# Accumulating kv = phi(k)ᵀ v per head on 32-column PE tiles instead of per pair of heads on 64-column tiles

## Chip, cores, metric

One core of one Trainium2 chip. The metric is the device time in microseconds of one execution, as a median over runs; 2% is the line between "same" and a difference. A *pair* below is a weight load and its matmul; *entry* is the time from the start of the last matmul ahead of a block to the first start in it.

## The reference, cut to what matters

A gated mix of a linear-attention block (2048 tokens, 32 heads of 32) and a feed-forward on one selected row. The change touches this part:

```python
pq, pk = phi(q), phi(k)                       # phi(t) = where(t > 0, t + 1, exp(t)) + 1e-6
kv = jnp.einsum("bhsd,bhse->bhde", pk, v)     # per head: 32 x 32, summed over 2048 tokens
z  = jnp.einsum("bhsd->bhd", pk)              # per head: the sum of phi(k)
num = jnp.einsum("bhqd,bhde->bhqe", pq, kv)
den = jnp.einsum("bhqd,bhd->bhq", pq, z)[..., None] + 1e-6
```

z comes for free when v carries a column of ones.

## The kernel before

Tokens are taken in 16 tiles of 128. For each, k and v are projected (512-column matmuls, `unit_KV`), k goes through phi into `pk`, v into `vt`. Every fourth tile, the sums of four tiles of tokens are added up in one block (`unit_KVACC` four times):

```python
def kv_slot(g):                                    # g: 8 groups of 4 heads
    return kvacc[g // 4][:, 65 * (g % 4) : 65 * (g % 4) + 65]
...
vt_t[t] = kvp.tile([P, NG, 2, 65], BF, tag="vt", name=f"vt{t}")
nc.gpsimd.memset(vt_t[t][:, :, :, 64:65], 1.0)
...
def unit_KVACC(t):
    for g in range(NG):
        for h in range(2):                         # two heads at once, on a 64-column tile
            pe.matmul(kv_slot(g)[64 * h : 64 * h + 64, :], lhsT=pk_t[t][:, g * P + 64 * h : g * P + 64 * h + 64],
                      rhs=vt_t[t][:, g, h, :], start=False, stop=False, skip_group_check=True, tile_position=(0, 64 * h))
    del pk_t[t], vt_t[t]
...
for t in range(4):
    unit_KVACC(t)
for t in range(4, NT):
    for nb in range(4):
        unit_KV(t, nb)
        if nb == 1 and t > 4 and t % 4 == 0:
            for t0 in range(t - 4, t):
                unit_KVACC(t0)
        ffn_step(GU_AFTER.get((t, nb), 0))         # gate/up matmuls of the selected row, 32-column tiles
```

Two heads share a matmul, so half of each 64x64 product (head a's k with head b's v) is computed and never used. Each matmul has its own weight load (`lhsT`), so a block is 64 pairs of load and matmul. Just ahead of the first block stands `rps`, the router (32 matmuls on 32-column tiles); after the third stand gate/up matmuls, after the fourth `yps`, all on 32-column tiles.

## Time and profile before

| | before |
|---|---|
| time | 251.35 us (250.92 to 251.53) |
| TensorE busy | 244.6 us of 251.4 |
| four kv blocks in the chain | 4 x 1.14 us |
| matmuls and weight loads into `kvacc` | 256 and 256 |

The prediction below shows the lines that say so.

The timeline of DVE after the last block (start, length, engine, operation, out<-in, shapes, count):

```profile
159.04 0.22 DVE L80 COPY zcol<-kvacc 128x4 f32<-128x4 f32 x2
159.18 0.42 DVE L80 CAST kvbd<-kvacc 128x256 bf16<-128x256 f32 x1
...
159.97 0.42 DVE L80 TENSOR_TENSOR zc<-mzc,zcol 128x256 bf16<-128x256 f32 x1
...
160.47 0.36 DVE L80 CAST kvbd<-kvacc 128x256 bf16<-128x256 f32 x1
```

These five operations bring the sums out of PSUM. The first reader of `zc` starts at 162.3 us.

### The profile page before, as it was taken

The page shows a single profiled execution, that of the slowest core. Times are in us where ns is not written, and L with a number is a line of the kernel's source. Part 1 is how long each engine was busy: PE and PEld are TensorE (multiplying, and loading weights), DVE is VectorE, ACT ScalarE, POOL GpSimd, SP SyncE. Part 2 cuts the span into 40 slices and gives each one's busy share as a digit, 9 for nine tenths or more (in the row PEclk, how much of TensorE's full clock was granted, in tenths as well). Part 3 has the DMA queues.
Part 4 walks back from the last instruction along what each step waited for, and adds up shares of the span by engine and source line. Part 5 has one row for each costly group of instructions (what it writes and reads, how often), then busy time and mean ns, then how long its engine had stood idle before and what let it go on. Part 6 is the DMA issues. An engine that isn't in the chain of part 4 may idle for free.

```text
span 251.4 us, 4171 instructions
## 1 busy us (share of the span) xinstructions
PE 244.6 (97%) x1576; PEld 112.0 (45%) x1602; DVE 163.3 (65%) x257; ACT 125.7 (50%) x200; POOL 51.8 (21%) x102
## 2 busy tenths in 40 slices
PE   8999999999999999999999999999999999999994
PEld 3444445444444534444544444444444444444442
DVE  0036005244999469699699993585888999953442
ACT  2068334455455355545535644568888633333210
POOL 5000002010000100000033000210666689950000
PEclk9999999999999999999999999999999999999999
DMA  6999990008999992489699996130000564454122
GB/s 191 308 344 215 258 341 18 0 5 269 356 348 287 331 288 68 146 297 328 215 310 314 429 349 146 52 132 7 4 0 0 158 220 146 152 183 139 71 83 83
DMA packets 47242, 47.73 MB, mean 190 GB/s; under 512 B 18732, under 2 KB 35380, under 8 KB 47160
## 3 DMA queue, kind: packets, MB, share of 16 engines
q1 hardware_dynamic: 46552, 46.29, 60.2%
q0 software_dynamic: 640, 1.19, 1.6%
q8 instruction: 12, 0.20, 0.3%
q14 instruction: 6, 0.05, 0.1%
q10 hardware_dynamic: 32, 0.00, 0.0%
HBM read 39.34 MB, written 8.40 MB: 190 GB/s over the span
## 4 chain that ended last, share of the span: by engine, by line
PE 95%; DMA 2%; issue 1%; SPq 0%; DVE 0%; DVEq 0%
PE ps L80 87%; PE first L80 3%; DMA xnat<-in_A_x_dram 2%; PE kvacc L80 2%; PE dps L80 1%; PE rps L80 1%; PE pm L80 1%; PE pst L80 0%; PE gps L80 0%; SPq L80 0%; DVE ot L80 0%; PE yps L80 0%; PE xs_ps L80 0%; DVEq L747 0%; PE pt L80 0%
## 5 line engine op out<-in xcount | busy, mean ns | idle before, releaser
L80 PE MATMUL ps<-wkv,xT 128*128 128x512 bf16 x468 | 105.6, 379 | 0.6
L80 PEld LDWEIGHTS <-xT 128*128 128x128 bf16 x512 | 49.9, 99 | 60.9 <-issue 3.0
L80 PE MATMUL ps<-xT,wq 128*128 128x512 bf16 x248 | 57.5, 379 | 0.7 <-issue 0.5
L80 PE MATMUL ps<-m_sb,pq_all 128*128 128x512 bf16 (+2 forms) x259 | 55.3, 372 | 0.3
L80 ACT ACTIVATE u<-ps 128x512 f32<-128x512 f32 x60 | 35.8, 597 | 36.8 <-PE ps L80 36.1
L80 ACT ACTIVATE e<-u 128x512 f32<-128x512 f32 x64 | 40.3, 630 | 2.0
L650 POOL TENSOR_TENSOR pq_all<-pq_all,rb 128x512 bf16<-128x512 bf16 x32 | 36.6, 1172 | 14.4 <-DVE rb L80 14.0
L80 PEld LDWEIGHTS <-pq_all 128*128 128x128 bf16 x264 | 25.5, 98 | 30.2 <-issue 0.4
L80 PEld LDWEIGHTS <-wq 128*128 128x128 bf16 x256 | 24.3, 98 | 30.2 <-issue 2.1
L80 DVE SCALAR_TENSOR_TENSOR pq_all<-ps,e 128x512 bf16<-128x512 f32 x32 | 21.9, 686 | 23.8 <-ACT e L80 23.7
L80 DVE SCALAR_TENSOR_TENSOR gacc<-wt,hcol,gacc 128x1024 f32<-128x1024 bf16 x27 | 34.6, 1282 | 3.8 <-DMA wt<-in_B_w_down_dram 3.3
L80 ACT CAST vt<-ps 128x512 bf16<-128x512 f32 x32 | 18.8, 587 | 31.6 <-PE ps L80 31.6
L80 DVE SCALAR_TENSOR_TENSOR ot<-ps,gate,xg 128x512 bf16<-128x512 f32 (+2 forms) x33 | 23.8, 733 | 15.0 <-PE ps L80 14.2
L80 ACT ACTIVATE xg<-xt,omg 128x1024 f32<-128x1024 bf16 x16 | 18.1, 1145 | 25.9 <-DVE ot L80 25.9
L80 DVE SCALAR_TENSOR_TENSOR pk<-ps,e 128x512 bf16<-128x512 f32 x28 | 19.1, 686 | 7.5 <-ACT e L80 7.5
L209 POOL MEMSET vt<- 128x16 bf16 x16 | 2.4, 199 | 103.2 <-PE kvacc L80 102.6
L80 DVE STREAM_SHUFFLE rb<-rdp 128x512 f32<-128x512 f32 x32 | 22.8, 746 | 0.0
L80 DVE SCALAR_TENSOR_TENSOR gacc<-wt,xs_f,gacc 128x1024 f32<-128x1024 bf16 x14 | 17.4, 1279 | 0.5 <-DMA wt<-in_B_w_gate_dram 0.5
L80 PE MATMUL first<-wkv,xT 128*128 128x512 bf16 x31 | 8.9, 443 | 0.1
L80 DVE SCALAR_TENSOR_TENSOR pk<-first,e 128x512 bf16<-128x512 f32 x4 | 2.8, 692 | 9.3 <-ACT e L80 9.3
L80 DVE CAST r_bf<-rps 128x512 bf16<-128x512 f32 x1 | 0.7, 693 | 12.5 <-PE rps L80 12.5
L80 DVE RECIPROCAL rd<-dn 128x512 f32<-128x512 f32 x2 | 6.7, 3338 | 0.0
(104 smaller groups left out, 89.3 us busy)
## 6 DMA issues: line engine op xcount, KB each, us to landing
wt<-in_B_w_down_dram SPq DMA_DIRECT2D x14, 512.0 KB, 5.5
wt<-in_B_w_gate_dram SPq DMA_DIRECT2D x8, 512.0 KB, 7.3
wt<-in_B_w_up_dram SPq DMA_DIRECT2D x8, 512.0 KB, 8.6
xt<-xp SPq DMA_DIRECT2D x16, 256.0 KB, 3.0
out_dram<-ot SPq DMA_DIRECT2D x15, 256.0 KB, 2.0
wt<-in_B_w_gate_dram SPq DMA_DIRECT2D x8, 384.0 KB, 6.9
wt<-in_B_w_up_dram SPq DMA_DIRECT2D x8, 384.0 KB, 7.6
wkv<-in_A_wqkv_dram SPq DMA_DIRECT2D x8, 256.0 KB, 5.2
```

The costliest lines, as they stand in the source:

```text
L80: inst = fn(*a, **k)
L209: nc.gpsimd.memset(vt_t[t][:, :, :, 64:65], 1.0)
L650: nc.gpsimd.tensor_tensor(sl, sl, rb[:], op=ALU.mult)
```

## The change

Its intent: compute no cross terms. Each head gets a 32-column tile of its own, four run at a time, and streams 33 columns instead of 65; 8 x 33 = 264 columns fit one PSUM bank, so the evacuation is shorter too.

```diff
-        return kvacc[g // 4][:, 65 * (g % 4) : 65 * (g % 4) + 65]
+        return kvacc[0][:, 33 * g : 33 * g + 33]
...
-            for h in range(2):
-                pe.matmul(kv_slot(g)[64 * h : 64 * h + 64, :], lhsT=pk_t[t][:, g * P + 64 * h : g * P + 64 * h + 64],
-                          rhs=vt_t[t][:, g, h, :], ..., tile_position=(0, 64 * h))
+            for h in range(4):
+                pe.matmul(kv_slot(g)[32 * h : 32 * h + 32, :], lhsT=pk_t[t][:, g * P + 32 * h : g * P + 32 * h + 32],
+                          rhs=vt_t[t][:, g, h, :], ..., tile_position=(0, 32 * h))
...
+    acc8 = kvacc[0][:, 0:264].rearrange("p (g e) -> p g e", e=33)
+    dve.tensor_tensor(zc[:], mzc[:], acc8[:, :, 32:33].to_broadcast([P, NG, 32]), op=ALU.mult)
+    dve.tensor_copy(kvbd[:], acc8[:, :, 0:32])
```

(`vt` has the shape [P, NG, 4, 33], `kvbd` [P, NG, 32], and the two copies into `zcol` and the second copy into `kvbd` go.) The price is in the loop: 128 pairs of load and matmul in a block instead of 64.

More of the change, by code (lines that the diff above doesn't have):

```diff
@@ L98 @@
     omg = keep.tile([P, NT], F32)
-    kvbd = keep.tile([P, NG, 64], BF)
+    kvbd = keep.tile([P, NG, 32], BF)
     zc = keep.tile([P, NG, 32], BF)
@@ L207, in kv_open @@
             pk_t[t] = kvp.tile([P, D], BF, tag="pk", name=f"pk{t}")
-            vt_t[t] = kvp.tile([P, NG, 2, 65], BF, tag="vt", name=f"vt{t}")
-            nc.gpsimd.memset(vt_t[t][:, :, :, 64:65], 1.0)
+            vt_t[t] = kvp.tile([P, NG, 4, 33], BF, tag="vt", name=f"vt{t}")
+            nc.gpsimd.memset(vt_t[t][:, :, :, 32:33], 1.0)
     def kv_mm(ps, t, nb, c0, c1):
@@ L219, in kv_evac @@
         else:
-            act.copy(vt_t[t][:, 4 * (nb - 2) : 4 * (nb - 2) + 4, :, 0:64], ps[:].rearrange("p (g h e) -> p g h e", g=4, h=2))
+            act.copy(vt_t[t][:, 4 * (nb - 2) : 4 * (nb - 2) + 4, :, 0:32], ps[:].rearrange("p (g h e) -> p g h e", g=4, h=4))
     def unit_KV(t, nb):
@@ L229, in unit_KVACC @@
         for g in range(NG):
-            for h in range(2):
-                pe.matmul(kv_slot(g)[64 * h : 64 * h + 64, :], lhsT=pk_t[t][:, g * P + 64 * h : g * P + 64 * h + 64],
-                          rhs=vt_t[t][:, g, h, :], start=False, stop=False, skip_group_check=True, tile_position=(0, 64 * h))
+            for h in range(4):
+                pe.matmul(kv_slot(g)[32 * h : 32 * h + 32, :], lhsT=pk_t[t][:, g * P + 32 * h : g * P + 32 * h + 32],
+                          rhs=vt_t[t][:, g, h, :], start=False, stop=False, skip_group_check=True, tile_position=(0, 32 * h))
         del pk_t[t], vt_t[t]
@@ L286 @@
     ps_acc = ph1.enter_context(tc.tile_pool(name="ps_acc", bufs=1, space=PSUM))
-    kvacc += [ps_acc.tile([P, 512], F32, name=f"kvacc{i}") for i in range(2)]
+    kvacc += [ps_acc.tile([P, 512], F32, name=f"kvacc{i}") for i in range(1)]
     ps_red = ph1.enter_context(tc.tile_pool(name="ps_red", bufs=1, space=PSUM))
@@ L593 @@
     unit_Q(*q_units.popleft())
-    zcol = keep.tile([P, NG], F32)
-    for i in range(2):
-        acc4 = kvacc[i][:, 0:260].rearrange("p (g e) -> p g e", e=65)
-        dve.tensor_copy(zcol[:, 4 * i : 4 * i + 4], acc4[:, :, 64])
-    dve.tensor_tensor(zc[:], mzc[:], zcol[:].unsqueeze(2).to_broadcast([P, NG, 32]), op=ALU.mult)
-    for i in range(2):
-        acc4 = kvacc[i][:, 0:260].rearrange("p (g e) -> p g e", e=65)
-        dve.tensor_copy(kvbd[:, 4 * i : 4 * i + 4, :], acc4[:, :, 0:64])
+    acc8 = kvacc[0][:, 0:264].rearrange("p (g e) -> p g e", e=33)
+    dve.tensor_tensor(zc[:], mzc[:], acc8[:, :, 32:33].to_broadcast([P, NG, 32]), op=ALU.mult)
+    dve.tensor_copy(kvbd[:], acc8[:, :, 0:32])
     ph1.close()
@@ L662, in unit_kvT @@
                     pe.matmul(pt[c][32 * r : 32 * r + 32, 32 * hf : 32 * hf + 32],
-                              lhsT=kvbd[32 * c : 32 * c + 32, 4 * hf + r, 32 * (c % 2) : 32 * (c % 2) + 32],
+                              lhsT=kvbd[32 * c : 32 * c + 32, 4 * hf + r, :],
                               rhs=ident[32 * c : 32 * c + 32, 32 * c : 32 * c + 32],
```

## The prediction

> **What bounds the kernel now.** I read the page from the top: busy shares, slices, the chain that ended last, then the groups of TensorE.
>
> ```profile
> PE 244.6 (97%) x1576; PEld 112.0 (45%) x1602; DVE 163.3 (65%) x257; ACT 125.7 (50%) x200; POOL 51.8 (21%) x102
> PE   8999999999999999999999999999999999999994
> PEclk9999999999999999999999999999999999999999
> PE 95%; DMA 2%; issue 1%; SPq 0%; DVE 0%; DVEq 0%
> ```
>
> TensorE works from end to end at full granted clock, and the chain is TensorE for 95% of the span; no other engine has a stretch on it except the first load and the last store. So only TensorE's own time counts, nearly one for one, and work removed from DVE, ACT or POOL is worth nothing unless TensorE had waited for it. The next lines, from the groups of TensorE by shape, say how much of it the change touches, and the chain in order of time says what that costs in wall time:
>
> ```profile
> L80 PE MATMUL ps<-wkv,xT 128*128 128x512 bf16 x468 | 105.6, 379 | 0.6
> L80 PE MATMUL kvacc<-vt,pk 128*64 128x65 bf16 x256 | 4.8, 196 | 0.0
> L80 PE MATMUL rps<-xT,wrg_pad 128*32 128x512 bf16 x32 | 1.9, 380 | 0.0
> ```
> ```profile
> 36.13 1.84 PE rps L80 x32
> 37.97 1.14 PE kvacc L80 x64
> ...
> 58.21 0.30 PE xs_ps L80 x9
> ...
> 82.15 1.14 PE kvacc L80 x64
> ...
> 123.29 1.14 PE kvacc L80 x64
> ...
> 157.11 1.14 PE kvacc L80 x64
> 158.25 0.57 PE yps L80 x8
> ...
> 165.19 0.22 PE pt L80 x32
> ```
>
> The columns are start, length, engine, tile, line and count. The accumulation of kv is four blocks of 64 matmuls, 1.14 us each, 4.56 us in all: 1.8% of the span. That is the whole stake, so even removing it altogether would not reach 2% (5.0 us). A block's 1.14 us is 17.8 ns for a matmul although one lasts 196 ns, because they are pipelined and two 64-column tiles run side by side. The single starts in the trace show it: the two of a pair start 3 to 10 ns apart, and pairs follow at 29 and 35 ns alternately (the longer after an odd head group). The block takes 1014 ns from first to last start, then some 126 ns until the next group starts. A block is entered 309 ns after the start of the matmul before it, where 512-column matmuls otherwise follow at 216 ns.
>
> **What the Trainium skill says.** "TensorEngine Tiling (Array Packing)", Instruction Overhead, gives each matmul about 60 cycles of overhead and says that one with a free dimension of 1 takes as long as one of 60, and warns against taking a tiling factor from a dimension that is already small. Here 65 columns, just above that, become 33, below it. The trace agrees in the one place that shows it: the nine 1-column matmuls into xs_ps start 25 ns apart (one gap 38).
>
> "TensorE: Matmul & The Clock Gate", Wait — 56ns, not 53.3ns?, says that start-to-start is never below about 25 ns, and that decoding in microcode takes about 62 ns for each matmul. This trace goes below both: 17.8 ns averaged over 64 matmuls into kvacc, 3 to 4 ns between matmuls of different tiles. I therefore read the 25 ns as a floor for one tile, not for the engine; no row here shows it for a 32-column tile.
>
> "TensorEngine Tiling (Array Packing)", Key Properties, says that changing the tiling mode drains TensorE. The trace agrees: 309 instead of 216 ns on entry.
>
> "PSUM — Partial Sum Buffer", PSUM bank collisions raise a hardware error, quotes that different column tiles may access one bank at the same time on disjoint partitions. The trace agrees: rps is four 32-column tiles in one bank, and its groups of four 512-column matmuls follow at 216 ns, the same as one full matmul. So one bank for all sums is no brake.
>
> **The change, part by part.**
>
> (1) Matmuls. Order of instructions: 64 weight loads and 64 matmuls in a block become 128 and 128 (TensorE's list goes from 3176 to 3688 rows). Streamed columns for a tile: before 32 matmuls of 65 columns, after 32 of 33. The pitch of one tile is what counts if issue keeps up. From 512 columns in 216 ns, a column is 0.42 ns, plus some 2.5 ns fixed: 65 columns give 29.6 ns (the trace's 29; odd groups 35), 33 columns would give 16.3, and odd groups perhaps 22. The floor of 25 ns stands above that. With 25: 31 x 25 + about 10 for the last group = 785 ns instead of 1014, so 0.23 us less in a block, 0.92 us in four. Without the floor: 31 x 19 + 10 = 600, 0.41 us less in a block, 1.65 in four.
>
> (2) Mode switches. Three neighbours of the blocks are already 128x32: rps before the first, the gate/up matmuls (xs_pad) after the third, yps after the fourth. Those switches go: 309 becomes about 216 ahead of the first block, and the 126 after the third and fourth can shrink to some 30. Estimate 0.1 us each, 0.3 us in all; yps is fp32, so its share is the least sure.
>
> (3) DVE at the end of the first phase: two copies into zcol (152 ns each) and one of two copies into kvbd (390 ns) go, 0.7 us. zc was done at 160.4 us and its first user starts at 162.3; kvbd was done at 160.8 and is used at 165.1. Nothing waits: 0.
>
> (4) One of two memsets of a bank (485 ns, at 24.5 to 25.6 us) goes: off the path, 0. The ones column of vt is 32 elements a partition instead of 16, on POOL, which is 21% busy: 0. ACT's copies into vt keep 512 elements (587 ns) with runs of 32 instead of 64; ACT is 50% busy and TensorE never waited for vt: 0, even were they 10% longer.
>
> Sum: -0.92 - 0.3 = -1.2 us with the floor, 250.1; -1.95 without, 249.4.
>
> **Rivals.**
>
> (A) Issue becomes the bound. The block holds 256 instructions instead of 128. For: before the change the block needed 1014 / 128 = 7.9 ns for each instruction, and nothing in the trace runs a longer list faster. pt is 32 pairs of tiny matmuls at 3.3 ns a pair, but that is only 64 instructions, which could all have been queued during the long matmuls ahead of it; and its very last matmul came 22 ns late, as if the queue had run dry. Against: the alternation 29/35 by group shows that the old block was bound by its tiles and not by issue, and after the third block 128 kvacc instructions and then 64 of the gate/up matmuls went by without a gap. If issue were 8 ns an instruction and some 64 were queued at the start (an estimate from pt), with 0.3 us of filling during the entry gap, the other 192 take 1.54 - 0.31 = 1.23 us: 0.22 us more a block, 252 in the end. At 12 ns: 2.0 us a block, +1 us each, 255. For over 2% slower it would have to be above 13 ns.
>
> (B) The bound of a tile does not fall: the weight load and matmul of one 32-column tile alternate at the old 32 ns. Then time is unchanged but for the switches: 251.0. Against: the load of 64 columns fitted in 29 ns, and 32 columns should need no longer.
>
> (C) Instruction fetch. The instruction queue moved 12 packets and 0.20 MB, so 16 KB each, about one for 256 rows, each taking about 1 us. A new block is one such page. If two page borders fall within one block TensorE could wait up to 1 us; with blocks of 256 rows that is unlikely, and rows 373 to 628, the first, hold one border.
>
> (D) A new wait: the whole sum in one bank means that the copies wait for the last matmul of all groups, as they did before, since each bank was finished only by the last tile of tokens. 0.
>
> **Range and chances.** The mechanism with floor gives 250.1, without it 249.4, (B) 251.0, (A) 252 to 255. I give the first two together 0.55, (B) and mixtures near it 0.2, (A) 0.25. The median of that is a little above the floor case: 250.4. Range 249.2 to 253.5, which also holds the spread of the runs before (250.92 to 251.53). Faster by over 2% (under 246.3) would need more than the whole accumulation to vanish: 0.01. Slower by over 2% (over 256.4) needs a block of 2.4 us: 0.05.
>
> **What would show it.** In the chain by time, kvacc should be four pieces of x128, 0.9 us each (0.7 without the floor, 1.14 in (B), 1.3 to 2 in (A)). Single starts: groups of four, 3 to 4 ns within, 25 ns from group to group; in (A) an even 8 to 12 ns between instructions with no groups of four, after a quick first quarter of the block. The first block should be entered at about 216 ns instead of 309, and the gate/up matmuls should follow the third at under 50 ns. The rest of the chain should keep its lengths, DVE should lose 1.2 us and nobody should wait for kvbd or zc. Wrong would be: a gap of TensorE inside a block, a wait for vt, or a piece elsewhere that grew.

## More of the kernel before

In the chain that ended last, in order of time (start in us, length, engine, tile, count), the first matmuls and the gate/up matmuls after the third block:

```profile
7.72 5.75 PE first L80 x21
...
124.43 1.74 PE ps L80 x33
```

## The result

251.09 us (250.99 to 251.37, 4 runs) against 251.27 us for the kernel before; ratio 0.9995 (0.9978 to 1.0013): the same.

The page of the changed kernel: busy times, instruction fetch, and the shares of the chain.

```profile
PE 242.7 (97%) x1832; PEld 111.6 (45%) x1858; DVE 162.6 (65%) x253; ACT 126.0 (51%) x200; POOL 53.0 (21%) x102
...
q8 instruction: 14, 0.23, 0.4%
...
PE 95%; DMA 2%; issue 1%; SPq 1%; DVE 0%; DVEq 0%
```

Its group of kv matmuls (tile size, streamed shape, count, busy us, mean ns), and the chain in order of time:

```profile
L80 PE MATMUL kvacc<-vt,pk 128*32 128x33 bf16 x512 | 5.0, 184 | 0.0
```
```profile
6.59 4.69 PE first L80 x21
...
33.95 1.84 PE rps L80 x32
35.79 1.12 PE kvacc L80 x128
...
79.95 1.21 PE kvacc L80 x128
...
121.16 1.19 PE kvacc L80 x128
122.35 1.65 PE ps L80 x33
...
154.94 1.13 PE kvacc L80 x128
156.07 0.49 PE yps L80 x8
```

Still nothing but TensorE in the chain, and no idle time at a kv matmul. The four blocks took 1.12, 1.21, 1.19 and 1.13 us, 4.65 in all, instead of 4.56: half the columns for twice the instructions came out even. The neighbours gave a little: 1.74 to 1.65 us for the gate/up matmuls after the third block, 0.57 to 0.49 us for `yps`. (The profiled span is 2.3 us shorter, 249.1 against 251.4, but that is no gain: the profiled run of the kernel before took 253.06 us, more than any of its timed runs. Half of it is the first matmuls, 4.69 us against 5.75, and the other half lies before them. From the start of the last 512-column matmul ahead of `rps` to the start of the last matmul of the kernel it is 211.96 us before and 211.88 after, and the timed runs agree with that.)

How one new block goes can be seen in the gaps between the starts of its matmuls, in ns, here the fourth; a weight load belongs to each:

```
(entry 310) 3 3 4 28  4 3 4 14  4 3 5 13  4 3 5 14  3 3 6 13  4 2 6 13  4 3 6 12  4 3 6 14
9 8 8 9  10 9 8 8  9 8 9 8  8 8 9 8  8 9 9 7  9 8 8 9  8 8 10 7  8 9 8 8  ... to the end
```

The first 32 matmuls (28 in the first block) come in groups of four, after the first group one every 25 ns. The other 96 come one by one, 8.3 ns apart; in the first three blocks, a gap of some 31 ns stands in that part every 32 matmuls. That is the picture that the experiments had to explain: is the second part set by the supply of instructions (theory I), by the one bank (B), or by the tiles themselves (C)? (Theory I is the prediction's rival A; the letters B and C are the experiments' own here, not the prediction's.)

### The profile page after: what moved, and what is told of

The parts are those of the page before. It is cut to its first block, busy times and chain, and to the rows that moved or that the text cites. A ratio compares the mean times of both kernels' runs of the same rounds, so it can differ in the third digit from the quotient of the medians.

```text
span 249.1 us, 4680 instructions
## 1 busy us (share of the span) xinstructions
PE 242.7 (97%) x1832; PEld 111.6 (45%) x1858; DVE 162.6 (65%) x253; ACT 126.0 (51%) x200; POOL 53.0 (21%) x102
## 3 DMA queue, kind: packets, MB, share of 16 engines
q0 software_dynamic: 640, 1.19, 1.6%
## 4 chain that ended last, share of the span: by engine, by line
PE 95%; DMA 2%; issue 1%; SPq 1%; DVE 0%; DVEq 0%
PE ps L80 88%; PE first L80 3%; PE kvacc L80 2%; DMA wkv<-in_A_wqkv_dram 2%; PE dps L80 1%; PE rps L80 1%; PE pm L80 1%; SPq L80 1%; PE gps L80 0%; DVE ot L80 0%; PE yps L80 0%; PE xs_ps L80 0%; DVEq L742 0%; PE pt L80 0%; PE hps L80 0%
## 5 line engine op out<-in xcount | busy, mean ns | idle before, releaser
L209 POOL MEMSET vt<- 128x32 bf16 x16 | 3.5, 306 | 100.2 <-PE kvacc L80 99.8
L80 PE MATMUL first<-wkv,xT 128*128 128x512 bf16 x31 | 7.3, 382 | 0.1
```

The source lines that it names most:

```text
L80: inst = fn(*a, **k)
L209: nc.gpsimd.memset(vt_t[t][:, :, :, 32:33], 1.0)
```

## The experiments

Four kernels on one chip, with before at 251.11 us (7 runs).

### 1. Two banks again

```diff
-        return kvacc[0][:, 33 * g : 33 * g + 33]
+        return kvacc[g // 4][:, 33 * (g % 4) : 33 * (g % 4) + 33]
```

> The changed kernel, with its sums again in two PSUM banks (head groups 0 to 3 and 4 to 7), all else as changed. Theory I (issue): in the changed kernel the first 32 or so pairs of weight load and matmul in a block of 128 come out of a full queue at 25 ns a group of four, and all the others at the rate at which TensorE is given instructions, 8.3 ns a pair plus some 23 ns every 32 pairs; banks do not matter, so blocks stay 1.0 to 1.1 us from first to last start and the time is that of the changed kernel, 250.9 to 251.3 us, ratio to before 0.998 to 1.001. Rival B (bank): four tiles that add into one bank get in each other's way; then two banks, of which each still takes four groups in a row, change little within a run of 16 matmuls, but the hand-over would show as a shorter gap, and a block below 0.95 us would speak for B.

Measured: 251.09 us, ratio 1.0004 (0.9984 to 1.0024). In the chain:

```profile
35.69 1.12 PE kvacc L80 x128
...
154.83 1.13 PE kvacc L80 x128
```

The same lengths as with one bank, and the gaps are again 25 ns a group for 32 matmuls, then 8 to 9 ns each. So the part of the change that put all sums into one bank cost and saved nothing here. Alone this is a weak test of rival B, as 16 matmuls in a row still go to one bank; experiment 3, which keeps the one bank and has 25 ns a group throughout, rules it out.

### 2. Twice the columns, the same list of instructions

```diff
-                          rhs=vt_t[t][:, g, h, :], ...
+                          rhs=vt_t[t][:, 4 * g + h : 4 * g + h + 2, :], ...   # 66 columns; slots of 66 in two banks
```

> The changed kernel with 66 columns streamed for each head instead of 33 (the head's own 33 and the next 33, which land in unused columns of its slot; slots of 66 in two banks), so the tiles have twice the work and the list of instructions is the same; the result stays right. Theory I (issue): a tile needs 66 columns x 0.42 + 2.5 = 30 ns, still below four pairs at 8.3 = 33 ns, so only the first 32 pairs of a block slow down (25 to 30 or 35 ns a group, 8 groups): +0.04 to 0.08 us a block, blocks 1.1 to 1.2 us, time +0.2 to +0.4 us against the changed kernel, 251.2 to 251.6. Rival C (tile): if the streaming of a tile or its weight load sets the 33 ns, twice the columns add 13.8 ns to each of 32 groups, 0.44 us a block, 1.8 us in all: 252.9 us, ratio 1.0065.

Measured: 251.47 us, ratio 1.0024 (1.0001 to 1.0048), result right.

```profile
36.01 1.21 PE kvacc L80 x125
...
80.26 1.42 PE kvacc L80 x125
...
155.55 1.16 PE kvacc L80 x122
```

(The trace holds all 128 matmuls of each block; the chain leaves out a few of them.) Double the streaming cost 0.38 us, in the range of theory I, not 1.8. In the fast part the groups now follow at about 30 ns, as 66 columns need, and it lasts longer; after it the pairs come at 8 to 9 ns on average as before. The second block grew most, by a single gap of 125 ns whose cause I did not pursue; one like it, of 86 to 120 ns, stands in the second block of experiments 3, 8 and 10 too. So the slow part did not wait for the columns streamed through the tiles. The other half of rival C, the weight load, is not tested here; experiments 3 and 10 do that.

### 3. The same instructions, dealt out among long matmuls

```diff
     for c in range(KC):
         for j in range(4):
             pe.matmul(rps[32 * j : 32 * j + 32, :], ...)
+        unit_KVACC(c // 2, 4 * (c % 2), 4 * (c % 2) + 4)      # 16 kv matmuls
...                                                           # (cut: the old calls for these two blocks go)
+            if nb == 1 and t == 12:
+                for i in range(8):
+                    ffn_step(1)
+                    unit_KVACC(8 + i // 2, 4 * (i % 2), 4 * (i % 2) + 4)
```

> The changed kernel with two of the four blocks dealt out among long matmuls of the same tiling mode: 16 kv matmuls after each group of four of the router's (first block), and after each group of four of the gate/up matmuls (third block). The same instructions in another order, but the queue can fill while 512-column or 384-column matmuls run. Theory I (issue): in these blocks all groups of four follow at about 25 ns, so the router and first block together take about 1.84 + 0.8 = 2.65 us instead of 2.96, third block and gate/up about 0.3 us less than before the move: 0.6 us less in all, about 250.5 us, ratio 0.997. Rivals B and C (bank, tile): the pairs cost 8.3 ns wherever they stand, and the time stays at 251.1; with a loss of up to 0.2 us if the long matmuls and the short ones hinder each other.

Measured: 250.55 us, ratio 0.9981 (0.9960 to 1.0001). The chain at the first block and at the third:

```profile
34.49 0.09 PE kvacc L80 x16
34.59 0.22 PE rps L80 x4
34.81 0.10 PE kvacc L80 x16
...
121.44 0.10 PE kvacc L80 x16
121.53 0.17 PE ps L80 x4
121.70 0.09 PE kvacc L80 x16
```

16 kv matmuls now take 0.09 to 0.10 us every time, 25 ns a group, to the last group. From the start of `rps` to the first matmul after the block it is 2.66 us; in the changed kernel it was 2.97, and theory I had said 2.65. So the 8.3 ns belong neither to the matmuls nor to the tiles: they appear when more than some 32 pairs follow each other without a long matmul, in whose time the queue can fill. This is the run that decides for theory I, by its trace (the time alone, 0.9960 to 1.0001, would not): bank and tiles are out, and the supply of instructions is left as the bound. Which stage of that supply it is, no run here tells.

One rival with the same look is that matmuls are held back behind the array, by earlier ones that have not finished. No run varies that, but the weight loads of the changed kernel speak against it (loads and matmuls matched in order of their starts). In the fast part of a block, after the first group of four, a load starts 23 to 27 ns before its matmul, some 2 ns after the matmul before it on its own tile. In the slow part it starts 4 to 10 ns before its matmul, just after the matmul that stands before it in the list, though its tile had been ready for it some 24 ns earlier. So the loads come late too, and each pause of 31 ns falls between a load and its own matmul.

### 4. Eight matmuls in a row on one tile

```diff
-        for g in range(NG):
-            for h in range(4):
+        for h in range(4):
+            for g in range(NG):
```

> The changed kernel with the loops over heads and groups exchanged, so eight matmuls in a row go to the same 32-column tile. My prediction took 25 ns as a floor between two matmuls of one tile, not of the engine. If that is so, every start is 25 ns after the one before, issue (8.3 ns a pair) no longer matters, a block takes 124 x 25 + 4 x 8 = 3.1 us instead of 1.1, and the time is 8.2 us longer: 259.3 us, ratio 1.032. If a 32-column tile has no such floor, a matmul takes 33 columns, 16.3 ns: block 2.1 us, time 255.1. If the four tiles gave nothing at all, the time would stay at 251.

Measured: 254.97 us, ratio 1.0152 (1.0132 to 1.0172); a block takes 1.99 to 2.00 us from first to last start. By its time alone this looks like the second case, no floor and 16.3 ns a matmul. The timeline says otherwise. This is the end of the third block, where the list of instructions has all 128 kv matmuls ahead of the gate/up matmuls:

```profile
125.02 0.30 PE L80 MATMUL kvacc<-vt,pk 128*32 128x33 bf16 x9
125.15 0.34 PE L80 MATMUL ps<-wt,xs_pad 128*32 128x384 bf16 x3
125.17 0.23 PE L80 MATMUL kvacc<-vt,pk 128*32 128x33 bf16 x3
125.25 0.97 PE L80 MATMUL ps<-wt,xs_pad 128*32 128x384 bf16 x17
```

Three gate/up matmuls start before the last three kv matmuls. By the order of the list, these three are for the fourth tile and the gate/up matmuls for the three tiles that are done (the trace does not name the tile of a matmul). The end of the fourth block looks the same, with three matmuls of `yps`. So matmuls of different column tiles overtake each other, and the eight of one tile overlap with the next eight. The last four starts on the fourth tile are 25, 27 and 25 ns apart: the floor of a tile stands. My expectation failed because it took the starts to be in program order.

Four more kernels, with before at 251.57 us (11 runs).

### 5. The kernel before with 33 columns

```diff
-                pe.matmul(kv_slot(g)[64 * h : 64 * h + 64, :], ..., rhs=vt_t[t][:, g, h, :], ...)
+                pe.matmul(kv_slot(g)[64 * h : 64 * h + 64, 0:33], ..., rhs=vt_t[t][:, g, h, 0:33], ...)
```

> The kernel before (64-column tiles, 64 pairs of weight load and matmul in a block) with only the first 33 of the 65 columns streamed: the result is wrong on purpose (half of the sums are missing). It takes the shorter streams of the change without its doubled list of instructions. Theory I (the old block was bound by the columns of its tiles, the new one by issue at 8.3 ns a pair): two pairs take 16.7 ns to issue, below the 25 ns cadence of a tile that the fourth experiment showed, so pairs of matmuls follow at 25 ns, without the alternation of 29 and 35; block 31 x 25 + 5 = 780 ns instead of 1014, 0.93 us less in four: 250.2 us, ratio 0.9963. Rival: the old block was bound by issue too, 15.8 ns a pair; then it stays at 1014 ns and 251.1 us.

Measured: 251.42 us, ratio 0.9998 (0.9979 to 1.0016). Its output is wrong, which doesn't matter for the time.

```profile
35.96 1.13 PE kvacc L80 x64
```

1.13 us against 1.14: a miss. The 29 and 35 ns became an even 32, and the block stayed at 1012 ns. Halving the streamed columns is worth nothing in the old block, so I had read its bound wrongly.

### 6. The kernel before with slots on even columns

```diff
-        return kvacc[g // 4][:, 65 * (g % 4) : 65 * (g % 4) + 65]
+        return kvacc[g // 4][:, 66 * (g % 4) : 66 * (g % 4) + 65]
```

> The kernel before with the slots of the sums 66 instead of 65 columns apart, so each starts on an even fp32 column in the bank; the result is right. The pairs of matmuls in the old block follow at 29 and 35 ns alternately, 35 after an odd head group, whose slot starts on an odd column. If the odd start in PSUM costs the 5 to 6 ns: all pairs at 29 to 30 ns, block 0.92 us instead of 1.014, 0.36 us less in four, 250.75 us. If it is the streamed operand (which starts at an odd multiple of 4 bytes for odd groups), the alternation stays and so does the time.

Measured: 251.55 us, ratio 1.0006 (0.9987 to 1.0025), blocks 1.14 us, the alternation unchanged. Where a slot starts in the bank does not matter here. What makes the 29 and 35 is left open; with experiment 5 in hand it does not matter, as the mean of 32 ns is set by something else.

### 7. A third block dealt out

```diff
+        for i in range(GU_AFTER.get((t, "end"), 0)):
+            ffn_step(1)
+            if t == 8:
+                unit_KVACC(4 + i)          # the second block, here instead of after nb == 1 of the same tile
```

> As the third experiment, and the second block too is dealt out, among the gate/up matmuls at the end of the eighth tile of tokens, 32 kv matmuls after each of four groups. Theory I: the second block, 1.10 us with an entry of 309 instead of 216 ns and 110 ns to leave, becomes 32 groups at 25 ns without a change of mode of its own: about 0.45 us less than the third experiment (250.55), 250.1 us; ratio to before 0.996. If it stays at 250.5 or more, something waits for the later release of the kv operands of tokens 4 to 7, which would show as idle time of TensorE or in the evacuations of the ninth tile.

Measured: 250.53 us (250.16 to 252.11, 6 runs), ratio 0.9972 (0.9947 to 0.9997).

```profile
85.58 0.25 PE kvacc L80 x32
85.83 0.23 PE ps L80 x3
86.06 0.24 PE kvacc L80 x30
```

32 matmuls in 0.24 us after each group of gate/up (the chain leaves out a few). Over the stretch used above, from the last 512-column matmul ahead of `rps` to the last matmul, it is 211.02 us, against 211.38 in experiment 3 and 211.88 in the changed kernel. The median is 1.0 us below both before and the changed kernel of the same rounds; the ratio, which counts the one run of 252.11 us too, says 0.7 us against before (0.1 to 1.3). (The expectation compared with 250.55 on a chip where before ran in 251.11; here before ran in 251.57, so only differences within the rounds count.)

### 8. The changed kernel in the same rounds

> The changed kernel itself, in the same rounds as the others, to have a closer comparison. All theories: 251.1 us, ratio 0.999 to 1.001, and the trace as recorded: blocks with a quick first quarter.

Measured: 251.51 us, ratio 0.9997 (0.9980 to 1.0015). Its second block took 1.30 us where the first profile had 1.21, the others were alike.

Two last kernels, with before at 251.08 us (one of its 7 runs was slow and is left out of the ratios).

### 9. The kernel before with 33 columns and weights of 48

```diff
-  kv_slot(g)[64 * h : 64 * h + 64, 0:33], lhsT=pk_t[t][:, g * P + 64 * h : g * P + 64 * h + 64]
+  kv_slot(g)[64 * h : 64 * h + 48, 0:33], lhsT=pk_t[t][:, g * P + 64 * h : g * P + 64 * h + 48]
```

> The kernel before with 33 columns streamed, as in the fifth experiment, and with weights of 48 instead of 64 columns in the same 64-column tiles (wrong on purpose). The fifth experiment showed that the old block does not depend on the columns streamed: pairs of matmuls at 32 ns with 65 and with 33. New theory W (weight load): loading 64 columns sets those 32 ns, about 0.42 x 64 = 27 plus 5; then 48 columns take 0.42 x 48 + 5 = 25 ns, block 31 x 25 + 50 = 0.80 to 0.85 us instead of 1.012, 0.7 to 0.85 us less in four, 250.6 us if before is at 251.4. Rival F: a 64-column tile has a fixed cadence of 32 ns, or issue gives this tiling a pair of load and matmul every 16 ns; then the block stays at 1.01 us.

Measured: 249.99 us, ratio 0.9954 (0.9924 to 0.9983). Its output is wrong, which doesn't matter for the time.

```profile
36.04 0.92 PE kvacc L80 x64
...
154.52 0.92 PE kvacc L80 x64
```

The blocks fall from 1.13 to 0.92 us: 810 ns from first to last start, pairs of matmuls every 25 ns. The tile and the number of instructions are those of experiment 5, so neither a fixed cadence of 64-column tiles nor issue sets the 32 ns; the width of the weights does. The starts of the loads point to the load itself: in experiment 5 as here, a tile's next load starts some 2 ns after its matmul, and the matmul for it 30 ns after the load with 64 columns, 23 to 25 ns with 48. (Narrower weights also write fewer rows of the sums; no run separates the two. And 25 ns a group is the floor that weights of 32 and 16 columns show too, so what 48 columns alone would need stays open.) I take the old block to have been bound by its weight loads.

### 10. Narrow weights on 32-column tiles

```diff
-  kv_slot(g)[32 * h : 32 * h + 32, :], lhsT=pk_t[t][:, g * P + 32 * h : g * P + 32 * h + 32]
+  kv_slot(g)[32 * h : 32 * h + 16, :], lhsT=pk_t[t][:, g * P + 32 * h : g * P + 32 * h + 16]   # on experiment 3
```

> The third experiment (kv matmuls dealt out in two blocks, where groups of four follow at 25 ns) with weights of 16 instead of 32 columns in the same 32-column tiles (wrong on purpose: half of the rows of each sum are missing). If the 25 ns are a floor of the tile, they stay: groups of 16 in 0.09 to 0.10 us, time as the third experiment, 0.998 of before. If they are the weight load (0.42 x 32 + 11), they fall to about 18 ns (0.42 x 16 + 11, or 16.3 for 33 columns): pieces of 16 in 0.07 us, 0.15 us less in each of the two blocks. The blocks that are not dealt out stay at 8.3 ns a pair after the first 32 pairs in any case, if issue sets it.

Measured: 250.91 us, ratio 0.9993 (0.9971 to 1.0016). (Half of the sums are missing; the comparison with the reference did not notice.)

```profile
34.43 0.09 PE kvacc L80 x16
34.52 0.23 PE rps L80 x4
34.75 0.09 PE kvacc L80 x16
```

With half the weights a group of four still takes 25 ns: on a 32-column tile with 33 columns that is a floor and not the load. In the two blocks that stand alone the pairs still come at 8.3 ns after the first 32: with half the weights to load nothing changed there, so the load is not what the slow part waits for. (The time expected was that of experiment 3, 0.998 of before; the interval holds it, but holds no difference too.)

## Why the prediction was right or wrong

The call was right: "same" at 0.94, and 251.09 us lies in 249.2 to 253.5. What made it right is the size of the stake; the gain of 1.2 us that the main mechanism forecast did not come, and the range held the result because it was also wide enough for the rivals. That part is luck. The central 250.4 was 0.7 us too low, and the sum behind it does not hold in two of its steps.

**What bounds the kernel, and the stake.** Right. The change moved only what TensorE did in those 4.56 us and at their edges.

**Step 1, the matmuls.** This is the step that failed, by its premise "what counts if issue keeps up". The part with the floor was right: 25 ns a group in the fast part of each block, and wherever the supply keeps up (experiment 3). The Trainium skill's floor of about 25 ns ("TensorE: Matmul & The Clock Gate", Wait — 56ns, not 53.3ns?) is a floor of one column tile: in experiment 3 four tiles each keep 25 ns, so the engine starts a matmul every 6 ns. But only a quarter of the matmuls in a block ran at it. (The fixed 2.5 ns in this step come out of the trace before, where 512 columns take 216 ns from start to start and 128 columns 56; the alternation is coarser than 29 and 35, single gaps being 29, 33, 29, 35.) In place of 785 ns, blocks took 1010 to 1118 ns from first to last start, because 96 of 128 pairs came at 8.3 ns: 8 x 25 + 96 x 8.3 = 1.0 us, plus 23 ns for each longer gap in the first three blocks. The -0.92 us of this step became about zero.

**Rival A** was the right mechanism at half the size. I had weighed 8 to 12 ns for an instruction; it is 8.3 ns for a pair, so 4.2 for an instruction, after a fast part of 64 instructions, which is the number that I had guessed. At 4.2 ns the loss that I gave A (252 to 255 us) turns into a draw. The argument that I brought against A, that the old block was bound by its tiles, was true but did not bear on the new block with twice the instructions.

**The reading of the old block.** I worked out 29.6 ns from 65 columns and found it in the trace's 29. That was a coincidence that experiments 5 and 9 took apart: with 33 columns the block stays at 1012 ns, and with narrower weights it falls to 810. So the old kernel was bound by the width of its weights, by the evidence of the loads by loading 64 columns every 32 ns. The change removes that bound, but puts one of equal size in its place, and this is where the gain went.

**Step 2, the switches.** Right in part. The entry of the first block went from 309 to 206 ns; the gap after the third fell from 126 to 8 ns and after the fourth from 126 to 9. That is 0.34 us, close to the 0.3 estimated. Most of it was eaten by the blocks themselves: from first to last start the four took 1118 + 1101 + 1086 + 1010 = 4315 ns, where the old ones took 4 x 1014 = 4056. Of the whole sum 0.08 us was left (211.96 against 211.88).

**Steps 3 and 4.** Right. The timeline of DVE after the change:

```profile
156.88 0.41 DVE L80 TENSOR_TENSOR zc<-mzc,kvacc 128x256 bf16<-128x256 f32 x1
157.21 0.42 DVE L80 CAST kvbd<-kvacc 128x256 bf16<-128x256 f32 x1
```

Two operations instead of five, and the first user of `zc` starts at 160.0, about as long after the end of the last block as before (4.05 us by the chain, 4.13 before). DVE lost 0.7 us of busy time, less than the 1.2 that I had written. Nobody waited for either.

**Rivals B, C, D** (the prediction's letters). B (the old 32 ns stay) was near in time but wrong in cause: four pairs at 8.3 ns make 33. C, the instruction fetch: two more packets, and no gap of TensorE near 1 us in a block; the gaps of 31 ns every 32 pairs, and the varying length of the second block (1.21 and 1.30 us, single gaps of 86 to 125 ns in four of the runs), may belong to it, which stays open. (The traces have 3178 and 3690 records of TensorE's loads and matmuls; the prediction's 3176 and 3688 are each 2 short, which changes nothing.) D, the wait of the copies for one bank: 0, as the unmoved start after `zc` shows, and experiment 1.

## What to carry to other kernels

Before cutting matmuls into smaller tiles, count the instructions: here a run of pairs of weight load and matmul went at 8.3 ns a pair after its first 32, however little each had to do, so halving the work and doubling the list was a draw. Put such runs between long matmuls of the same tiling mode, where they are supplied in their shadow: for three of the four blocks that made this change worth 0.7 to 1.0 us, still far under 2%. And to name the bound of a group of small matmuls, vary the streamed columns and the width of the weights one at a time; a number that fits one of them may be chance.

## What the Trainium skill lacked or had wrong

- "TensorE: Matmul & The Clock Gate", The mechanism (in Part 3), says that matmuls start in strict program order, without reordering. Experiment 4 shows three gate/up matmuls starting ahead of three kv matmuls that stand before them in the list; by the list they are on other column tiles.
- The same page (Wait — 56ns, not 53.3ns?) gives about 25 ns as the least from start to start without saying there that it is for one tile, though its Part 3 has tiles starting some 4 ns apart. Here four 32-column tiles together started a matmul every 6 ns on average, each tile every 25 ns.
- No page has the sustained supply of small pairs of load and matmul: 8.3 ns a pair after the first 28 to 32, with a longer gap (31 ns) every 32 pairs in most blocks. What the skill has near it does not give this rate: on the same page about 81 ns for full-array pairs at 128 columns, 62 ns for each matmul decoded in microcode, and a queue of 64 entries, which would fit the fast part of 32 pairs; in "Runtime: NRT & Kernel Launch" some 20 cycles an instruction.
- "TensorE: Matmul & The Clock Gate", LDWEIGHTS (loading the stationary operand), gives columns / 1.2 ns, which would be 53 ns for 64 and 40 ns for 48 (estimates from its formula). Tiles of 64 columns took a new load and matmul every 32 ns with weights of 64 columns and every 25 ns with 48, and a matmul started 30 and 23 to 25 ns after its load.
- "TensorEngine Tiling (Array Packing)", Key Properties, says that a change of mode drains the array, but not what it costs: on entry from a 512-column matmul 309 instead of 216 ns from start to start, and 126 instead of 8 ns from the last kv matmul to the gate/up matmuls.
